# Sliding-window attention and a two-layer MLP on one core: a rewrite with other tiles, another normalisation and a scheduled order

## The chip, the cores and the metric

The kernel runs on one core of a Trainium2 chip. The metric is the device time of one execution in microseconds (us). Five engines work side by side, each through its own list of instructions in order: TensorE (PE; its weight loads are shown as PEld), VectorE (DVE), ScalarE (ACT), GpSimd (POOL) and SyncE (SP). DMA queues move data between the chip's main memory and the core's SBUF. Matmuls write to PSUM, 8 banks of 128 partitions by 2 KB.

## The reference

Inputs are q, k and v in f32, each 8 batches x 8 heads x 576 positions x 64 values, and the weights `w_in` (512 x 2048) and `w_out` (2048 x 512). Cut to what matters:

```python
scores = q @ k.T / 8
mask_plain = (rel >= 0) & (rel < 32)
mask_dil = (rel >= 0) & (rel < 128) & (rel % 4 == 0)
attn = softmax(where(mask, scores, -1e9))
x = (attn @ v) with the heads side by side
h = x @ w_in
out = maximum(0.01 * h, h) @ w_out
```

`rel` is the query's position less the key's. Heads 0 to 3 have the plain mask, heads 4 to 7 the dilated one, so a query sees 32 keys at most. There are 4608 tokens (8 x 576); the output is 4608 x 512 in f32.

## The kernel before

**Attention** (L213) takes a batch and a pair of heads at a time, 32 rounds in all. `load_and_transpose` loads 576 x 128 values of q and then of k through SP's queue in rows of 256 B, casts them to f16 on ACT (L182), transposes them with five matmuls against an identity (L185, L186) and copies them out of PSUM on DVE (L190). `load_v` (L193) has POOL clear a tile (L195), loads v by SP and casts it on ACT (L210). Scores are matmuls of 96 queries (plain) or 72 (dilated) against the 128 keys before them, one head at a time on 64 rows of the array (L236). ACT takes the exponential (L241), DVE multiplies by the mask (L248). The result times v goes into one PSUM tile (L252), and times a 128 x 64 tile of ones into another (L258), which holds the row sums on 64 partitions. DVE takes their reciprocal (L265) and multiplies (L279) into `xT`, which holds the attention's output, features on partitions.

**Weights** are loaded in f32 in the second round (L147), cast on DVE, and `w_in` is transposed (L160) and multiplied by `w_out` (L166) into `w_eff`, 0.01 of the product. The MLP uses max(h, 0.01h) = 0.99 relu(h) + 0.01h: the second part is `x @ w_eff`, without the hidden layer.

**The MLP** takes chunks of 512 tokens. An up group (L286) is four matmuls of 512 columns (L289) and then 0.99 relu on ACT (L301) or, one time in three, on DVE (L296). A down group (L306) is 16 matmuls with `w_out` (L310) and four with `w_eff` (L317), a copy on ACT (L324) and a store by SP (L325).

The order of the work is that of the program: after each round of attention at most six groups of the MLP are issued (L340), for chunks whose tokens are complete, and the rest at the end (L354).

Of the kernel before, what the change touches and what calls it, by code (L numbers as in the profile page):

```python
# [16 lines left out]
PAD = 128  # L18
POST = 128


def _mask_plain_np(S):
    krel = np.arange(128)[:, None]
    c = np.arange(S)[None, :]
    t = c // 96
    key = 96 * t - 32 + krel
    rel = c - key
    m = (key >= 0) & (rel >= 0) & (rel < WIN)
    return m.astype(np.float16)


def _mask_dil_np(S):
    krel = np.arange(128)[:, None]
    c = np.arange(S)[None, :]
    rem = c % 144
    tau = rem // 72
    ql = rem % 72
    uq = 72 * tau + ql
    uk = 72 * tau - 32 + krel
    m = (uk >= 0) & ((uq - uk) >= 0) & ((uq - uk) < WIN)  # L40
    return m.astype(np.float16)


class _QTile:

    __slots__ = (
        "half", "jl", "w", "ecol", "kstart", "kstep", "kcnt",
        "qstart", "qstep", "vslice",
    )

    def __init__(self, half, jl, w, ecol, kstart, kstep, kcnt, qstart, qstep, vslice):
        self.half = half
        self.jl = jl
        self.w = w
        self.ecol = ecol
        self.kstart = kstart
        self.kstep = kstep
        self.kcnt = kcnt
        self.qstart = qstart
        self.qstep = qstep  # L60
        self.vslice = vslice


def _plain_qtiles():
    res = []
    for t in range(6):
        res.append(
            _QTile(
                half=t // 3, jl=t % 3, w=96, ecol=96 * t,
                kstart=PAD + 96 * t - 32, kstep=1, kcnt=128,  # L70
                qstart=PAD + 96 * t, qstep=1, vslice=t,
            )
        )
    return res


def _dil_qtiles():
    res = []
    for r in range(4):
        for tau in range(2):  # L80
            j = 2 * r + tau
            res.append(
                _QTile(
                    half=r // 2, jl=2 * (r % 2) + tau, w=72,
                    ecol=144 * r + 72 * tau,
                    kstart=PAD + 4 * (72 * tau - 32) + r, kstep=4, kcnt=128,
                    qstart=PAD + 4 * (72 * tau) + r, qstep=4, vslice=j,
                )
            )
    return res  # L90
# [3 lines left out]
def kernel(  # L94
# [7 lines left out]
    out: bass.AP,  # L102
):
    nc = tc.nc
    ctx.enter_context(nc.allow_low_precision("fp16 intermediates, 1e-3 rel tol"))

    B, H, S, D = q.shape
    assert H == 8 and D == 64 and S == 576, (B, H, S, D)
    NTOK = B * S
    DMODEL = H * D  # L110
    DFF = moe_w_in.shape[1]
    NH = H // 2
    QTW = PAD + S + POST
    SCALE = float(1.0 / np.sqrt(D))

    plain_qt = _plain_qtiles()
    dil_qt = _dil_qtiles()

    mask_plain_d = nc.inline_tensor(_mask_plain_np(S), name="mask_plain").ap()
    mask_dil_d = nc.inline_tensor(_mask_dil_np(S), name="mask_dil").ap()  # L120

    cst = ctx.enter_context(tc.tile_pool(name="cst", bufs=1))
    big = ctx.enter_context(tc.tile_pool(name="big", bufs=1))
    ld = ctx.enter_context(tc.tile_pool(name="ld", bufs=2))
    att = ctx.enter_context(tc.tile_pool(name="att", bufs=2))
    epool = ctx.enter_context(tc.tile_pool(name="epool", bufs=3))
    moe = ctx.enter_context(tc.tile_pool(name="moe", bufs=2))
    pat = ctx.enter_context(tc.tile_pool(name="pat", bufs=5, space=bass.MemoryType.PSUM))
    pmo = ctx.enter_context(tc.tile_pool(name="pmo", bufs=3, space=bass.MemoryType.PSUM))

    ident = cst.tile([128, 128], FP16)
    make_identity(nc, ident)
    maskpl = cst.tile([128, S], FP16)
    nc.sync.dma_start(maskpl, mask_plain_d)
    maskdl = cst.tile([128, S], FP16)
    nc.sync.dma_start(maskdl, mask_dil_d)
    ones64 = cst.tile([128, 64], FP16)
    nc.gpsimd.memset(ones64, 1.0)

    n_fc = DMODEL // 128  # L140
    n_j = DFF // 128
    w_in_sb = big.tile([128, n_fc, DFF], FP16)
    w_out_sb = big.tile([128, n_j, DMODEL], FP16)

    w_eff_sb = big.tile([128, n_fc, DMODEL], FP16)

    def load_weights():  # L147
        for i in range(n_fc):
            wtmp = ld.tile([128, DFF], FP32, tag="wtmp_in")
            nc.sync.dma_start(wtmp, moe_w_in[i * 128:(i + 1) * 128, :])  # L150
            nc.vector.tensor_copy(out=w_in_sb[:, i, :], in_=wtmp)
        for j in range(n_j):
            wtmp2 = ld.tile([128, DMODEL], FP32, tag="wtmp_out")
            nc.sync.dma_start(wtmp2, moe_w_out[j * 128:(j + 1) * 128, :])
            nc.vector.tensor_copy(out=w_out_sb[:, j, :], in_=wtmp2)
        wT = big.tile([128, n_j, n_fc, 128], FP16)
        for j in range(n_j):
            tpw = pat.tile([128, 512], FP16, tag="ps", name="tpw")
            for i in range(n_fc):
                nc.tensor.transpose(tpw[:, 128 * i:128 * i + 128],  # L160
                                    w_in_sb[:, i, j * 128:(j + 1) * 128], ident)
            nc.scalar.copy(out=wT[:, j, :, :], in_=tpw[:, 0:512])  # L162
        for i in range(n_fc):
            weps = pat.tile([128, DMODEL], FP32, tag="ps", name="weps")
            for j in range(n_j):
                nc.tensor.matmul(weps, wT[:, j, i, :], w_out_sb[:, j, :],  # L166
                                 start=(j == 0), stop=(j == n_j - 1))
            nc.scalar.activation(out=w_eff_sb[:, i, :], in_=weps,
                                 func=AF.Copy, scale=0.01)

    xT = big.tile([128, n_fc, NTOK], FP16)

    def load_and_transpose(b, hp, src, tag):
        qld = ld.tile([128, 5, 128], FP32, tag=f"{tag}_ld")
        nc.gpsimd.memset(qld[64:128, 4, :], 0.0)  # L175
        for hh in range(2):
            h = 2 * hp + hh
            srcap = src[b, h, 0:512, :].rearrange("(T p) d -> p T d", p=128)
            nc.sync.dma_start(qld[:, 0:4, 64 * hh:64 * hh + 64], srcap)  # L179
            nc.sync.dma_start(qld[0:64, 4, 64 * hh:64 * hh + 64], src[b, h, 512:576, :])  # L180
        qldh = ld.tile([128, 5, 128], FP16, tag=f"{tag}_ldh")
        nc.scalar.copy(out=qldh, in_=qld)  # L182
        tp = pat.tile([128, 1024], FP16, tag="ps")
        for T in range(4):
            nc.tensor.transpose(tp[:, 128 * T:128 * T + 128], qldh[:, T, :], ident)  # L185
# [27 lines left out]
    def attention(b, hp):  # L213
# [11 lines left out]
        for half in range(2):  # L225
            sps = [pat.tile([128, 512], FP32, tag="ps", name="sps") for _ in range(2)]
            for qtile in qtiles:
                if qtile.half != half:
                    continue
# [52 lines left out]
    def moe_chunk_groups(tok0, ntok):  # L282
# [45 lines left out]
        for j in range(n_j):  # L328
            yield mk_j(j)
# [56 lines left out]
```

The softmax here doesn't subtract the row's maximum and nothing guards it: scores larger than these inputs give would overflow.

## Time and profile before

| | |
|---|---|
| median of 3 runs | 439.18 us (438.53 to 440.29) |
| span of the profiled execution, from its first to its last instruction | 436.9 us |
| instructions | 7886 |
| PE, DVE, ACT, POOL busy | 90%, 56%, 48%, 15% of the span |
| data moved by DMA | 50.11 MB in 137320 packets |

The profile gives the profiled execution by its span. The median is 2.3 us above it: what lies before the first instruction and after the last. Matmuls overlap, so a busy PE says that some matmul is under way. In tables of groups the columns are line, engine, operation, output and inputs with shapes, count | busy time in us, mean ns of one | idle time of the engine before them and what ended it.

### The profile page before, as it was taken

To read this page: it belongs to the slowest core of one execution; us is meant where nothing else is said; L and a number is where in the kernel's file an instruction comes from. 1 tells how busy PE (TensorE), PEld (TensorE's weight loads), DVE (VectorE), ACT (ScalarE), POOL (GpSimd) and SP (SyncE) were. 2 spreads that over 40 slices of the span, in tenths; PEclk is the share of its full clock that TensorE was granted. 3 is DMA by queue.
4 is the path that set the end of the run, shared out by engine and by line. 5 is a ranking of instruction groups with operands and counts; after the bars stand their busy time and mean duration, and the time that the engine had idled before them with its cause. 6 is when DMAs were issued, how large, how long until landed. Compare 5 with 4: busy or idle time off the path is not lost.

```text
span 436.9 us, 7886 instructions
## 1 busy us (share of the span) xinstructions
PE 392.7 (90%) x2768; PEld 193.7 (44%) x2768; DVE 244.9 (56%) x321; ACT 207.7 (48%) x412; POOL 67.6 (15%) x263
## 2 busy tenths in 40 slices
PE   1344975699999999999999999999999999999996
PEld 1223433344444544454454444445445444444442
DVE  0573326787667657756775678567766765200200
ACT  2504554464467447744764475457446521422411
POOL 4300112112112112211221121112110000000000
PEclk9996995699999999999999999999999999999999
DMA  5857766553555555635654554455441001001001
GB/s 119 255 185 251 225 165 145 115 123 78 153 130 113 142 151 134 149 107 131 153 115 114 140 118 99 132 135 118 120 122 53 2 26 48 26 25 66 7 24 74
DMA packets 137320, 50.11 MB, mean 115 GB/s; under 512 B 129856, under 2 KB 130112, under 8 KB 136768
## 3 DMA queue, kind: packets, MB, share of 16 engines
q1 hardware_dynamic: 137280, 49.61, 43.5%
q8 instruction: 22, 0.36, 0.3%
q14 instruction: 18, 0.15, 0.1%
HBM read 40.14 MB, written 9.44 MB: 113 GB/s over the span
## 4 chain that ended last, share of the span: by engine, by line
PE 82%; DVE 5%; ACT 4%; DMA 3%; SPq 3%; issue 2%; ACTq 0%; POOL 0%; POOLq 0%; DVEq 0%
PE ops L310 29%; PE hps L289 27%; PE ops L317 7%; PE opair L252 4%; PE tp L185 3%; PE sps L236 3%; PE den L258 3%; PE weps L166 2%; DVE bc_sb L265 2%; PE tp L186 2%; ACT eraw L241 2%; DMA wtmp<-in_moe_w_in_dram 2%; ACT wT L162 1%; SPq L179 1%; DVE em L248 1%
## 5 line engine op out<-in xcount | busy, mean ns | idle before, releaser
L289 PE MATMUL hps<-xT,w_in_sb 128*128 128x512 f16 x576 | 138.3, 386 | 5.4 <-DVE xT L279 4.7
L310 PE MATMUL ops<-w_out_sb,gt 128*128 128x512 f16 x576 | 135.0, 380 | 0.0
L265 DVE RECIPROCAL bc_sb<-den 128x288 f16<-128x288 f32 x64 | 120.6, 1926 | 19.3 <-PE den L258 19.1
L310 PEld LDWEIGHTS <-gt 128*128 128x128 f16 x576 | 53.5, 98 | 65.0 <-issue 3.1
L289 PEld LDWEIGHTS <-w_in_sb 128*128 128x128 f16 x576 | 52.3, 99 | 66.1 <-issue 10.6
L301 ACT ACTIVATE gt<-hps 128x512 f16<-128x512 f32 x99 | 58.9, 604 | 43.7 <-PE hps L289 43.5
L324 ACT COPY osb<-ops 128x512 f32<-128x512 f32 x36 | 21.1, 585 | 106.8 <-PE ops L317 106.8
L182 ACT CAST qldh<-qld 128x640 f16<-128x640 f32 x64 | 45.0, 730 | 23.6 <-DMA qld<-in_q_dram 10.0
L296 DVE TENSOR_SCALAR gt<-hps 128x512 f16<-128x512 f32 x45 | 30.8, 686 | 44.2 <-PE hps L289 44.2
L241 ACT ACTIVATE eraw<-sps 128x288 f16<-128x288 f32 x128 | 42.4, 419 | 22.0 <-PE sps L236 21.8
L190 DVE COPY qt<-tp 128x576 f16<-128x576 f16 x64 | 27.6, 454 | 36.8 <-PE tp L186 36.7
L210 ACT CAST v<-vld 128x512 f16<-128x512 f32 x64 | 37.6, 631 | 13.0 <-issue 9.4
L195 POOL MEMSET vld<- 128x512 f32 x64 | 33.2, 526 | 59.0 <-ACT v L210 56.9
L317 PE MATMUL ops<-w_eff_sb,xT 128*128 128x512 f16 x144 | 37.0, 379 | 0.0
L185 PE MATMUL tp<-ident,qldh 128*128 128x128 f16 x256 | 26.4, 229 | 11.5 <-ACT qldh L182 8.2
L175 POOL MEMSET qld<- 64x128 f32 x64 | 13.3, 207 | 151.0 <-ACT qldh L182 127.6
L279 DVE TENSOR_TENSOR xT<-opair,bc_sb 128x288 f16<-128x288 f32 x64 | 34.2, 604 | 0.0
L252 PE MATMUL opair<-em,v 128*64 128x72 f16 (+1 forms) x448 | 25.4, 208 | 7.4 <-DVE em L248 4.6
L252 PEld LDWEIGHTS <-v 128*64 128x64 f16 x448 | 20.3, 114 | 20.5 <-DVE em L248 14.4
L248 DVE TENSOR_TENSOR em<-eraw,maskdl 128x576 f16<-128x576 f16 x32 | 13.2, 455 | 28.3 <-ACT eraw L241 28.3
L185 PEld LDWEIGHTS <-qldh 128*128 128x128 f16 x256 | 18.4, 101 | 22.3 <-ACT qldh L182 8.5
L248 DVE TENSOR_TENSOR em<-eraw,maskpl 128x576 f16<-128x576 f16 x32 | 13.2, 455 | 23.8 <-ACT eraw L241 22.2
(25 smaller groups left out, 185.0 us busy)
## 6 DMA issues: line engine op xcount, KB each, us to landing
out_dram<-osb SPq DMA_DIRECT2D x36, 256.0 KB
qld<-in_q_dram SPq DMA_DIRECT2D x64, 128.0 KB
qld<-in_k_dram SPq DMA_DIRECT2D x64, 128.0 KB
vld<-in_v_dram SPq DMA_DIRECT2D x32, 160.0 KB
wtmp<-in_moe_w_in_dram SPq DMA_DIRECT2D x4, 1024.0 KB
wtmp<-in_moe_w_out_dram SPq DMA_DIRECT2D x16, 256.0 KB
vld<-in_v_dram SPq DMA_DIRECT2D x32, 104.0 KB
vld<-in_v_dram SPq DMA_DIRECT2D x32, 96.0 KB
```

The source lines that it names most:

```text
L182: nc.scalar.copy(out=qldh, in_=qld)
L185: nc.tensor.transpose(tp[:, 128 * T:128 * T + 128], qldh[:, T, :], ident)
L195: nc.gpsimd.memset(vld, 0.0)
L210: nc.scalar.copy(out=v1, in_=vld)
L241: nc.scalar.activation(out=eraws[hh][:, half * 288:half * 288 + 288], in_=sps[hh][:, 0:288], func=AF.Exp, scale=SCALE,)
L252: nc.tensor.matmul(opair[qtile.half][r0:r0 + 64, ocols], v1s[hh][:, qtile.vslice, :], ecols, start=True, stop=True,)
L265: nc.vector.reciprocal(out=bc_sb[:, half, :], in_=den[half][:, 0:288])
L279: nc.vector.tensor_tensor(out=outap, in0=opair[half][:, 0:288], in1=bc_sb[:, half, :], op=ALU.mult)
L289: nc.tensor.matmul(hps[:, 0:ntok], w_in_sb[:, i, j * 128:(j + 1) * 128], xT[:, i, tok0:tok0 + ntok], start=(i == 0), stop=(i == n_fc - 1),)
L301: nc.scalar.activation(out=gt[:, j, 0:ntok], in_=hps[:, 0:ntok], func=AF.Relu, scale=0.99)
L310: nc.tensor.matmul(ops[0:ntt, :], gt[:, j, tt:tt + ntt], w_out_sb[:, j, :], start=(j == 0), stop=False,)
L317: nc.tensor.matmul(ops[0:ntt, :], xT[:, i, tok0 + tt:tok0 + tt + ntt], w_eff_sb[:, i, :], start=False, stop=(i == n_fc - 1),)
```

## The change

The kernel is written anew.

- **Loads cast to f16.** q, k, v and both weights are loaded by DMAs that POOL issues and that turn f32 into f16 on the way, in rows of 256 B for q, k and v. Of batch 0 the first 96 tokens of each residue (see below) come in f32 rows of 1 KB through SP's and ACT's queues and are cast on DVE and ACT.
- **Tokens are kept by residue.** Position 4u + s is stored as (s, u). A unit of work covers 2 x 96 queries of two heads, 384 columns; a batch and a pair of heads has three units. There are 96 units.
- **The whole array.** q of two heads stands block-diagonal in `qbd`, with zeros beside it, so that one matmul over 128 rows gives the scores of both heads. v stands beside 64 columns of ones, so that one matmul gives the output on 64 partitions and the row sums on the other 64.
- **1/x as Exp(-Ln x)**, two passes on ACT. One set of ACT tables is loaded at the start.
- **The MLP** has no `w_eff`: ACT's Prelu with alpha 0.01 gives max(h, 0.01h). Its chunks are 384 tokens, 12 of them; chunks 3m and 3m + 1 need the first two units of every pair of heads of batches 2m and 2m + 1, chunk 3m + 2 the third units of both. The copy of the result goes to DVE.
- **The order** is not that of the program: each piece of work becomes a task with an engine, a time, a delay, its predecessors and a priority, and a list scheduler, run while the kernel is built, puts the tasks in order of their planned starts. Buffers used in turn ("rings") are predecessors too.

The core of the diff (lines removed are those printed above):

```diff
+    UK = U + PADK
+    tpb = [bank("tp", FP16)]
+    sps = [bank(f"sps{i}") for i in range(1)]
+    ops = [bank(f"ops{i}") for i in range(2)]
+    hps = [bank(f"hps{i}") for i in range(2)]
+    fps = [bank(f"fps{i}") for i in range(2)]
...
+    def load(queue, dst, src, n, size, deps=(), issue=None):
+        eng = {"SP": nc.sync, "ACTQ": nc.scalar, "POOL": nc.gpsimd}[queue]
+        cost = {"SP": 0.5, "ACTQ": 0.5, "POOL": 1.0}[queue] if issue is None else issue
+        return dma(queue, cost, rate(n, size), deps,
+                   lambda: eng.dma_start(dst, src))
...
+                tp.append(load("POOL", at(vp[slot], p0, p1, 0, [128, 24], [1, D]),
+                               dram(v, b * H * HS + (s - 32) * D,
+                                    [4 * D, 32], [96 * D, 24], [1, D]),
+                               768, 256, deps_p))
+        for tau in range(2):
+            for h in range(4):
+                td.append(load("POOL",
+                               at(vd[slot], 0, 128, (h * 2 + tau) * 512, [128, 4], [1, D]),
+                               dram(v, (b * H + 4 + h) * HS + tau * 16 * 4 * D,
+                                    [4 * D, 128], [D, 4], [1, D]),
+                               512, 256, deps_d))
+        v_ready[b] = (tp, td)
...
+        for half in range(2) if b == 1 else (2,):
+            h0, hn = (4 * half, 4) if half < 2 else (0, 8)
+            for name, src, dst in (("q", q, qn), ("k", k, kn)):
+                ts = [load("POOL", at(dst[slot], 0, 128, s * 512 + h0 * D, [D, hn], [1, D]),
+                           dram(src, (b * H + h0) * HS + s * D, [4 * D, 128], [HS, hn], [1, D]),
+                           128 * hn, 256, deps) for s in range(4)]
+                for i in ((half,) if half < 2 else (0, 1)):
+                    got[name, i] = ts
+            if half != 1:
+                for name, src, p0 in (("q", q, 0), ("k", k, 64)):
+                    got[name, "l"] = load(
+                        "POOL", at(lf[slot], p0, p0 + 64, 0, [D, H], [1, D]),
+                        dram(src, b * H * HS + 512 * D, [D, 64], [HS, H], [1, D]),
+                        512, 256, deps)
...
+        for name, src, dst, queue in (("q", q, q0f, "SP"), ("k", k, k0f, "ACTQ")):
+            t_f32[name, hp] = load(
+                queue, at(dst, 0, 96, hp * 512, [256, 2], [1, 256]),
+                dram(src, 2 * hp * HS, [4 * D, 96], [HS, 2], [1, 256]), 192, 1024)
...
+    def ones(i):
+        t_ones["p", i] = pool_op(
+            lambda: nc.gpsimd.memset(at(vp[i], 0, 128, D, [128, 24], [1, D]), 1.0), 1.5)
+        t_ones["d", i] = pool_op(
+            lambda: nc.gpsimd.memset(at(vd[i], 0, 128, D, [128, 32], [1, D]), 1.0), 2.0)
...
+    cuts = [0, 128, 256, 512, 1024, 1536, 2048]
...
+    for n in range(len(cuts) - 1):
+        load_w_in(n)
+        if n == 2:
...
+    load_qk(1, [])
+    load_v(1, [], [])
+    ones(1)
+    for n in range(4):
+        t = load("POOL", at(w_out, 0, 128, n * 4 * DM, [DM, 4], [1, DM]),
+                 dram(moe_w_out, n * 4 * 128 * DM, [DM, 128], [128 * DM, 4], [1, DM]),
+                 512, 2048)
+        for j in range(4 * n, 4 * n + 4):
+            w_out_t[j] = t
+    ones(2)
...
+                def pe(src=src, tp=tp, pos=pos, lanes=lanes, to=to, tw=tw):
+                    nc.tensor.transpose(
+                        at(tp, 0, 128, to + 128, [tw, 4], [1, 32]),
+                        lf[lanes][:, hp * 128:hp * 128 + 128],
+                        con[:, 128 * pos:128 * pos + 128])
+                    for s in range(4):
+                        nc.tensor.transpose(
+                            tp[:, to + s * tw:to + s * tw + 128],
+                            src[lanes][:, s * 512 + hp * 128:s * 512 + hp * 128 + 128],
+                            ident)
...
+                                out=at(qbd[slot], 64 * hh, 64 * hh + 64, hh * S, [1, S]),
+                                in_=at(tp, 64 * hh, 64 * hh + 64, 0, [1, S]))
...
+                    ka = at(kt[slot], 0, 128, 128 * t, [1, 128])
+                    qa = at(qbd[slot], 0, 128, 24 * t, [S, 2], [U, 4], [1, 24])
+                nc.tensor.matmul(st[:, 192 * i:192 * i + 192], ka, qa, start=True, stop=True)
...
+                  lambda: nc.scalar.activation(out=et, in_=st[:, 0:384], func=AF.Exp, scale=SCALE),
+                  prio + 0.1)
...
+                        va = at(vp[b % NV], 0, 128, (h * 6 + t) * 128, [1, 128])
+                    c = 192 * i + 96 * hh
+                    nc.tensor.matmul(ot[:, c:c + 96], va, et[:, c:c + 96],
+                                     start=True, stop=True)
...
+        t_l = add("ACT", 0.37, 0.2, [t_v] + r_old,
+                  lambda: nc.scalar.activation(out=rt, in_=ot[64:128, 0:384], func=AF.Ln),
+                  prio + 0.2)
...
+        t_r = add("ACT", 0.37, 0.2, [t_l],
+                  lambda: nc.scalar.activation(out=rt, in_=rt, func=AF.Exp, scale=-1.0),
+                  prio + 0.2)
...
+                    out=at(xt[m % 2], p0, p0 + 64, base + e, *o_),
+                    in0=at(ot, 0, 64, c, *i_), in1=at(rt, 0, 64, c, *i_), op=ALU.mult)
...
+            for i in range(NI):
+                nc.tensor.matmul(ht[:, 0:384],
+                                 w_in[:, i * DFF + j * 128:i * DFF + j * 128 + 128],
+                                 at(xt[m % 2], 0, 128, i * 1152 + x0, [1, 384]),
+                                 start=(i == 0), stop=(i == NI - 1))
...
+                  lambda: nc.scalar.activation(out=gt[c % 2][:, j * 384:j * 384 + 384],
+                                               in_=ht[:, 0:384], func=AF.Prelu, alpha=0.01),
...
+                for j in range(4 * p, 4 * p + 4):
+                    nc.tensor.matmul(ft, gt[c % 2][:, j * 384 + tt * 128:j * 384 + tt * 128 + 128],
+                                     w_out[:, j * DM:j * DM + DM],
+                                     start=(j == 0), stop=(j == NJ - 1))
...
+        t_c = add("DVE", 0.62, 0.25, [pieces[-1]] + o_old,
+                  lambda: nc.vector.tensor_copy(out=ob, in_=ft), -1000)
...
+        for p0, tok, n in rows(c, tt):
+            dep = [t_c]
+            o_users.append(load("SP", dram(out, tok * DM, [4 * DM, n], [1, DM]),
+                                ob[p0:p0 + n, :], n, 2048, dep))
...
+    order = plan.run()
...
+    with tc.manual_schedule():
+        nc.scalar.preload_act_table_set("natural_log_exp_and_others")
+        for t in order:
+            t.fn()
```

## Rows read from the trace of the kernel before

**Rows 1.** Busy time by stretch: columns named in the second line

```profile
core 0: us, PE busy (x) PEld busy (x) DVE busy (x) ACT busy (x) POOL busy (x), PEclk, DMA share, GB/s
0.00:88.00 88.00, 48.71 (x370) 27.09 (x370) 42.24 (x59) 36.41 (x71) 17.44 (x69) 0.86 0.66 183
88.00:433.00 345.00, 343.77 (x2400) 166.56 (x2398) 202.68 (x263) 170.70 (x340) 50.11 (x194) 1.00 0.39 98
...
66.00:77.00 11.00, 5.22 (x50) 3.02 (x51) 7.66 (x9) 5.13 (x10) 2.86 (x11) 0.53 0.65 146
11.00:22.00 11.00, 4.00 (x41) 2.73 (x41) 6.70 (x10) 6.00 (x14) 3.72 (x14) 1.00 0.85 257
```

**Rows 2.** The chain of waits, 28 to 76 us: start, us, what

```profile
30.00 7.41 DMA wtmp<-in_moe_w_in_dram
...
45.07 10.67 PE weps L166 x48
```

**Rows 3.** The chain of waits, 333 to 437 us: start, us, what

```profile
343.61 0.24 PE den L258 x2
...
344.82 0.22 PE tp L185 x4
345.05 0.13 PE tp L186
...
350.06 0.65 PE sps L236 x16
...
352.12 0.38 PE opair L252 x8
...
371.03 13.81 PE hps L289 x64
384.84 3.45 PE ops L310 x16
388.29 0.86 PE ops L317 x4
```

**Rows 4.** Groups of instructions, shapes kept apart

```profile
L265 DVE RECIPROCAL bc_sb<-den 128x288 f16<-128x288 f32 x64 | 120.6, 1926 | 19.3 <-PE den L258 19.1
...
L301 ACT ACTIVATE gt<-hps 128x512 f16<-128x512 f32 x99 | 58.9, 604 | 43.7 <-PE hps L289 43.5
...
L279 DVE TENSOR_TENSOR xT<-opair,bc_sb 128x288 f16<-128x288 f32 x64 | 34.2, 604 | 0.0
L195 POOL MEMSET vld<- 128x512 f32 x64 | 33.2, 526 | 59.0 <-ACT v L210 56.9 <-DMA qld<-in_q_dram 2.2
L296 DVE TENSOR_SCALAR gt<-hps 128x512 f16<-128x512 f32 x45 | 30.8, 686 | 44.2 <-PE hps L289 44.2
L190 DVE COPY qt<-tp 128x576 f16<-128x576 f16 x64 | 27.6, 454 | 36.8 <-PE tp L186 36.7
...
L248 DVE TENSOR_TENSOR em<-eraw,maskdl 128x576 f16<-128x576 f16 x32 | 13.2, 455 | 28.3 <-ACT eraw L241 28.3
...
L182 ACT ACT_TABLE_LOAD x1 | 1.3, 1283 | 5.6 <-DMA qld<-in_q_dram 5.6
```

**Rows 5.** Timeline of SP's queue, 5 to 16 us: start, us, what

```profile
5.77 0.51 SPq L180 DMA_DIRECT2D qld<-in_k_dram  x1
6.33 0.59 SPq L179 DMA_DIRECT2D qld<-in_q_dram  x1
```

**Rows 6.** The page's part on DMA queues: packets, MB, share of 16 engines

```profile
q1 hardware_dynamic: 137280, 49.61, 43.5%
```

**Rows 7.** Timeline of ACT, 340 to 343 us: start, us, what, idle before

```profile
341.27 1.32 ACT L241 ACTIVATE eraw<-sps 128x288 f16<-128x288 f32 x4 [0.93 <-PE sps L236]
```

**Rows 8.** Timeline of the last microseconds: start, us, what

```profile
433.27 0.58 ACT L324 COPY osb<-ops 128x512 f32<-128x512 f32 x1 [3.73 <-PE ops L317]
433.88 0.33 SPq L325 DMA_DIRECT2D out_dram<-osb  x1
```

More of the change, by code (lines that the diff above doesn't have):

```diff
@@ L9 @@
 from concourse._compat import with_exitstack
-from concourse.masks import make_identity
 FP16 = mybir.dt.float16
@@ L44 @@
[L44 to L74, printed above, removed]
@@ L113 @@
-    QTW = PAD + S + POST
+    NP = H // 2
+    NI = DM // 128
+    NJ = DFF // 128
+    U = S // 4
     SCALE = float(1.0 / np.sqrt(D))
[L116 to L124, printed above, removed]
@@ L135 @@
[L135 to L169, printed above, removed]
@@ new lines, with load_w_in @@
+    t_vz = pool_op(lambda: nc.gpsimd.memset(vp[0][:, 0:D], 0.0), 0.2)
+    load_v(0, [t_vz], [])
+    t_ones = {}
+    def ones(i):
[3 more added lines that the diff above has]
+            lambda: nc.gpsimd.memset(at(vd[i], 0, 128, D, [128, 32], [1, D]), 1.0), 2.0)
+    ones(0)
+    cuts = [0, 128, 256, 512, 1024, 1536, 2048]
+    def load_w_in(n):
+        a, z = cuts[n], cuts[n + 1]
+        t = load("POOL", at(w_in, 0, 128, a, [DFF, NI], [1, z - a]),
+                 dram(moe_w_in, a, [DFF, 128], [128 * DFF, NI], [1, z - a]),
+                 512, 4 * (z - a))
+        for j in range(a // 128, z // 128):
+            w_in_t[j] = t
@@ new lines, with attend @@
+    for i in range(8):
+        add("PE", 0.43, 0.0, [t_warm],
+            lambda: nc.tensor.matmul(fps[0], warm[:, 0:128], warm, start=True, stop=True), -900)
+    def attend(b, part, units):
+        for hp in range(NP):
+            pr = rank(b, part, hp)
+            ev = transposes(b, hp, "all" if b else part, pr)
+            for u in units:
+                unit(b, hp, u, ev, pr)
+    acts_of, downs_of = {}, {}
+    for m in range(B // 2):
+        for b in (2 * m, 2 * m + 1):
+            if b >= 2:
+                load_qk(b, users_load.get(b - NQK, []))
+                load_v(b, users_v.get(b - NV, []), users_v.get(b - NV, []))
+            attend(b, 0, (0, 1, 2) if b else (0, 1))
+            if b == 0:
+                attend(0, 1, (2,))
+        x_free[m + 2] = []
+        for kind in range(3):
+            c = 3 * m + kind
+            acts = acts_of[c] = []
+            x_free[m + 2] += [up(c, j, acts) for j in range(NJ)]
+            gt_free[c] = downs_of[c] = []
+            for tt in range(3):
+                down(c, tt, acts, downs_of[c])
```

663 lines of the change are left out of this document (442 added, 221 removed).

## The prediction

> **What bounds the kernel now.** I read the busy time by stretch first. From 88 us on PE is busy for 343.77 of 345 us at the full granted clock of 1.00; DVE has 202.68 and ACT 170.70 [rows 1]. The chain of waits agrees: in that stretch it is almost nothing but matmuls, 64 of an up stage in 13.81 us, 16 of a down group in 3.45 us, so 215.7 ns for 512 columns with no gap [rows 3]. So a faster DVE alone would not move the end; fewer PE columns would. The first 88 us are another matter: PE is busy for 48.71 us of them, and its clock sinks to 0.53 between 66 and 77 us, about the lower level of 1.2 GHz, where it is busy less than half the time [rows 1]. There the chain goes through a weight load (7.41 us) and the 10.67 us of 48 matmuls for `w_eff` [rows 2]. The time is therefore a start of 88 us in which little PE work fits, 345 us of full PE, a tail of 4 us, and 2.3 us outside the span (436.9 against the median of 439.18).
>
> **PE's work after the change.** Prices by column come from [rows 3].
> - Up: 192 groups of four matmuls of 384 columns. 215.8 ns x 384/512 = 161.9 ns, so 124.3 us; the columns are those of before.
> - Down: 144 pieces of four matmuls, 36 x 3.45 = 124.2 us, as before.
> - Gone: 144 matmuls with `w_eff` (0.86 us for four: 31 us), the 64 that make it (222 ns each: 14 us) with their transposes (64 at 57 ns: 4 us), and 128 row-sum matmuls (0.12 us each: 15 us). Together 64 us.
> - Transposes: 28 rounds with ten, four rounds of batch 0 with sixteen. Four take 0.22 us now and the odd fifth 0.13; with 0.35 for five that is 19.6 us and, with 64 at 57 ns, 3.6 us.
> - Scores: 96 units of 384 columns. Sixteen of 72 columns take 0.65 us now, 41 ns each, but two heads run on two halves of the rows. The new form streams one head's zeros under the other's values, so it pays for all columns: 384/512 x 215.8 = 162 ns, 15.5 us.
> - Values: 80 units with four matmuls of 96 columns, 16 with eight of 48. Eight of 72 take 0.38 us, 47 ns each, so 0.19 and 0.38 us: 21 us. That the weights are twice as wide is unpriced in the trace; with a 128-column transpose as the upper price, 57 ns, it is 4.5 us more.
>
> Sum: 308 us. The steady part of before holds 343.77 us of PE and the whole 392.66; the new whole is less than the old steady part.
>
> **The other engines, beside PE.** ACT gets 96 Exp, 96 Ln, 96 Exp and 192 Prelu, all of 384 columns. Four Exps of 288 take 1.32 us [rows 7], so by proportion 0.44 us for 384: 211 us. DVE gets 96 copies out of PSUM at 454 ns, 96 masks at not more than 455, 192 products at not more than 604 and 36 copies at about 686 [rows 4]: at most 228 us. Both stay under PE's 308, but ACT, near 75% of the steady part, is the next in line. Where ACT is late, up groups wait for PSUM (below).
>
> The 64 reciprocals cost 1,926 ns each for 288 columns [rows 4], 6.7 ns a column. Kept on DVE for 96 units of 384 they would be 247 us, on top of 228: DVE would be the bound at about 475 us. Two passes on ACT are 0.88 us a unit. The Trainium skill, "ScalarE: Activation LUTs", section "What it computes", says to leave reciprocals to VectorE. By that rule this kernel would end near 490 us, by the rows it is better not followed here; the new kernel doesn't use ScalarE's own reciprocal, about whose accuracy the page warns.
>
> **The loads, and the start.** This is the part that the trace doesn't show: no DMA of before is issued by POOL, and none casts. What must arrive before the first down group can begin, in POOL's order: v of batch 0 (20 DMAs, 7,136 rows), `w_in` (6, 3,072), the rest of batch 0's q and k (8, 4,096), q and k of batch 1 (18, 9,216), its v (12, 7,168), `w_out` (4, 2,048). That is 68 DMAs with 32,736 rows. Batches 2 to 7 have 22 DMAs with 16,384 rows each; in all 131,040 rows.
> - POOL's time, lower end: SP's price, 0.51 to 0.59 us a DMA whether it has 64 rows or 512 [rows 5]: 68 x 0.55 = 37 us. Upper end: POOL works through a DMA row by row. Its memset takes 526 ns for 512 elements a partition, 1.03 ns an element [rows 4]. With four such steps a row it would be 4.1 ns, 135 us. I take two steps, one for the source and one for the destination: 2.06 ns a row, 67 us. In the queue stand also the memsets of ones (3,584 elements a batch buffer, two of them before `w_out`) and of 512 zeros, 7.9 us. With 2.7 us to land (the last store leaves at 434.2, the span ends at 436.9 [rows 8]), `w_out` is there at about 78 us.
> - The DMA engines' time: 137,280 packets took 43.5% of 16 engines over 436.9 us [rows 6], so 22.1 ns on one and 1.38 ns on all 16. 27,616 small rows take 38 us; 10.0 MB of weights and f32 rows at the best rate seen, 257 GB/s [rows 1], 39 us: 77 us. If all 17 MB went at 257 GB/s it would be 66 us.
>
> I take 72 us, between 66 and 78. Before that PE can do batch 0's attention (8 us), chunk 0's up stage (10.4 us) and what has come of batch 1's attention (about 4 us): 22 us. Values also wait for the ones, which stand behind 20 DMAs. The remaining 286 us then run without a load in the way, if POOL keeps ahead: a batch's 16,384 rows are 33.8 us of POOL and 22.6 us of the DMA engines, against 308/8 = 38.5 us of PE. The cover is 5 us thin on POOL; if it goes, POOL is late next.
>
> **Sum.** 72 + 286 = 358 us; the last copy (0.69 us, by L296's price), four stores of 0.33 us at SP and 2.7 us to land: 363 us of span; with 2.3 us outside, **365 us**. The PSUM clearings, the masks' load and the eight casts of batch 0 lie in the wait for the loads and cost nothing; without that wait the casts would be some 4 us of ACT and DVE.
>
> **Rivals.**
> 1. *POOL is the bound, and the kernel is slower.* Place: POOL's queue, all through. After batch 7's loads come its attention (12 us), chunks 10 and 11 (41 us) and the tail (5 us), so the time is 75.6 us (with memsets of 11.6, landing, start and 2.3 outside) plus 131,040 times the price of a row. It passes 439 us from 2.8 ns a row on, 2.7 steps of the memset's; at four steps it is 615 us. For it: nothing in the trace excludes four steps, and the rows are many and short. Against: SP's issue hardly grows from 64 rows to 512 [rows 5]. Chance 0.15. The Trainium skill, "DMA: Bandwidth & Descriptors", sections "Issuing engine by pattern" and "SWDGE vs HWDGE vs iDMA", speaks against the change here: descriptors of a DMA issued by GpSimd are computed by a program on its cores, one pair per operation, and the path of SP and ACT is generally faster, though only GpSimd's can cast. No run here shows such a DMA yet.
> 2. *PE waits in its order.* There are two banks for up groups where three were shared, one for scores and one for transposes. An up group takes 0.65 us and its Prelu some 0.5 (L301 takes 604 ns for 512 columns [rows 4]); with an Exp or Ln of 0.44 in front of it the bank is late by about 0.25 us. If that meets half of the 192 groups it is 24 us, 389 us in all; down pieces and attention between two up groups speak against it. Chance 0.14.
> 3. *The loads come faster.* Half as many bytes are written as read. With everything 1.4 times as fast `w_out` would land near 52 us, and the time be 345 us. Against: only rates up to 257 GB/s are seen. Chance 0.15.
> 4. *The single set of tables doesn't hold.* If Prelu were not in the set of Exp and Ln, each change would cost a table load of 1,283 ns [rows 4]; two for each of 192 Prelus are 493 us on ACT, so about 700 us. Chance 0.02.
>
> **Chances.** The forecast (357 to 380 us) 0.52, a time between 405 and 437 us 0.02. Faster by over 0.5% (about what a measurement of this kernel can tell from no change): 0.52 + 0.15 + 0.14 + 0.02 = 0.83. Slower: 0.15 and most of 0.02, so 0.16; 0.01 between. The range takes in rivals 2 and 3 and the bounds of the start, 335 to 420 us; it leaves out rivals 1 and 4 and a little below 335.
>
> **What would show it.** Right: PE below five tenths until some 70 us, then nine, clock 1.00; the first down matmul (512 columns with `w_out`) at 70 to 80 us; up matmuls at 162 ns and down at 216 in the chain; PE's busy time near 310 us; one table load; DVE and ACT each under 80%. The forecast is wrong if PE pauses for loads in every batch, with POOL's queue full throughout (rival 1), if its chain shows Prelu before up groups (rival 2), or if the first down matmul comes before 55 us (rival 3).

## The result and the profile after

The changed kernel takes **356.55 us** (median of 4 runs, 356.06 to 357.09), the kernel before in the same session 439.74 us (438.53 to 441.66): a ratio of 0.8112, interval 0.8087 to 0.8137. The profiled execution took 356.06 us, its span 354.3.

From the page: busy time by engine, then PE's busy share and its granted clock in 40 slices, each in tenths.

```profile
PE 320.3 (90%) x2368; PEld 191.4 (54%) x2368; DVE 174.4 (49%) x446; ACT 228.9 (65%) x485; POOL 161.1 (45%) x212
...
PE   4446866689999999999999999999999999999994
...
PEclk9555995599999999999999999999999999999999
```

Busy time by stretch, which answers to [rows 1]:

```profile
core 0: us, PE busy (x) PEld busy (x) DVE busy (x) ACT busy (x) POOL busy (x), PEclk, DMA share, GB/s
0.00:20.00 20.00, 9.87 (x58) 5.48 (x59) 10.66 (x30) 5.67 (x10) 16.34 (x28) 0.71 1.18 135
20.00:40.00 20.00, 11.82 (x80) 7.25 (x78) 8.77 (x27) 12.18 (x27) 15.98 (x22) 0.61 1.28 139
40.00:60.00 20.00, 14.40 (x131) 10.10 (x130) 12.07 (x33) 11.78 (x26) 18.97 (x25) 0.82 1.67 100
60.00:80.00 20.00, 15.07 (x118) 9.23 (x118) 12.77 (x36) 14.89 (x33) 16.28 (x19) 0.75 1.37 151
...
77.40:346.00 268.60, 268.60 (x1988) 159.41 (x1986) 131.32 (x327) 185.52 (x394) 95.03 (x123) 1.00 0.96 79
```

The picture is that of before with less of it: a start in which PE has gaps and a low clock, and then a stretch in which PE is busy without a gap. In it ACT has 185.52 of 268.60 us (69%), DVE 49%. In the start the granted clock falls to 0.50, the lower level of 1.2 GHz, in stretches where PE is idle for a large part of the time (10 to 30 us, where it is busy 8.80 of 20 us, and parts of 50 to 70, where it is busy 11.73 of 20). The start is about 77 us instead of 88, the full stretch 272 us instead of 345.

The chain of waits at the seam (start, us, what):

```profile
68.58 8.44 DMA qn<-in_q_dram
...
77.06 0.36 PE ops L536 x8
...
79.15 1.30 PE hps L607 x8
80.45 0.86 PE fps L646 x4
```

Eight up matmuls take 1.30 us (162 ns each), four down matmuls 0.86. The step that names the load of `qn` at 68.58 is an inference from semaphores: the matmul at 77.06 reads no q, and DVE's products of an earlier unit, whose output bank it may reuse, end at 76.91 us. So the chain's way through the start is taken with care below. The end, from the timeline:

```profile
337.79 11.39 PE L646 MATMUL fps<-w_out,gt 128*128 128x512 f16 x52
...
349.21 0.69 DVE L654 COPY osb<-fps 128x512 f32<-128x512 f32 x1 [2.76 <-DMA out_dram<-osb]
```

The last matmul ends at 349.18 us and the last copy starts right behind it.

Groups that answer to [rows 4, 7] (busy, mean ns, idle before):

```profile
L614 ACT ACTIVATE gt<-hps 128x384 f16<-128x384 f32 x192 | 93.4, 490 | 69.3 <-PE hps L607 67.0
L513 ACT ACTIVATE ee<-sps 128x384 f16<-128x384 f32 x96 | 46.8, 487 | 14.9 <-PE sps L508 14.4
L565 ACT ACTIVATE rc<-ops 64x384 f32<-64x384 f32 x96 | 46.1, 486 | 15.2 <-PE ops L551 11.4
L568 ACT ACTIVATE rc<-rc 64x384 f32<-64x384 f32 x96 | 49.2, 519 | 2.0
L586 DVE TENSOR_TENSOR xt<-ops,rc 64x192 f16<-64x192 f32 x192 | 67.1, 349 | 37.3 <-ACT rc L568 34.7
```

The reciprocal of one unit of 384 columns is now 486 + 519 ns on ACT.

### The profile page after: what moved, and what is told of

The parts are those of the page before. It is cut to its first block, busy times and chain, and to the rows that moved or that the text cites. A ratio compares the mean times of both kernels' runs of the same rounds, so it can differ in the third digit from the quotient of the medians.

```text
span 354.3 us, 6469 instructions
## 1 busy us (share of the span) xinstructions
PE 320.3 (90%) x2368; PEld 191.4 (54%) x2368; DVE 174.4 (49%) x446; ACT 228.9 (65%) x485; POOL 161.1 (45%) x212
## 4 chain that ended last, share of the span: by engine, by line
PE 76%; POOL 12%; DMA 10%; DVE 0%; issue 0%; SPq 0%; POOLq 0%
PE fps L646 33%; PE hps L607 32%; DMA w_in<-in_moe_w_in_dram 4%; POOL vd L233 3%; PE tp L397 3%; PE ops L551 3%; PE sps L508 3%; DMA qn<-in_q_dram 2%; DMA vp<-in_v_dram 2%; POOL vp L233 2%; POOL vd L319 1%; POOL qn L233 1%; POOL vp L317 1%; POOL kn L233 1%; POOL w_out L233 1%; POOL w_in L233 1%
## 5 line engine op out<-in xcount | busy, mean ns | idle before, releaser
L607 PE MATMUL hps<-xt,w_in 128*128 128x384 f16 x768 | 153.5, 330 | 1.3 <-DVE xt L586 1.2
L646 PE MATMUL fps<-w_out,gt 128*128 128x512 f16 x576 | 146.2, 381 | 0.0
L614 ACT ACTIVATE gt<-hps 128x384 f16<-128x384 f32 x192 | 93.4, 490 | 69.3 <-PE hps L607 67.0
L607 PEld LDWEIGHTS <-w_in 128*128 128x128 f16 x768 | 72.2, 99 | 48.8 <-issue 4.2
L586 DVE TENSOR_TENSOR xt<-ops,rc 64x192 f16<-64x192 f32 x192 | 67.1, 349 | 37.3 <-ACT rc L568 34.7
L513 ACT ACTIVATE ee<-sps 128x384 f16<-128x384 f32 x96 | 46.8, 487 | 14.9 <-PE sps L508 14.4
L565 ACT ACTIVATE rc<-ops 64x384 f32<-64x384 f32 x96 | 46.1, 486 | 15.2 <-PE ops L551 11.4
L527 DVE TENSOR_TENSOR ee<-ee,con 128x384 f16<-128x384 f16 x96 | 34.3, 358 | 42.7 <-ACT ee L513 40.9
L233 POOL DMA_DIRECT2D vd<-in_v_dram x64 | 47.5, 747 | 9.1 <-DMA vp<-in_v_dram 2.1
L568 ACT ACTIVATE rc<-rc 64x384 f32<-64x384 f32 x96 | 49.2, 519 | 2.0
```

What stands on the lines that cost most here:

```text
L233: lambda: eng.dma_start(dst, src))
L513: lambda: nc.scalar.activation(out=et, in_=st[:, 0:384], func=AF.Exp, scale=SCALE),
L527: nc.vector.tensor_tensor(out=io, in0=io, in1=mk, op=ALU.mult)
L565: lambda: nc.scalar.activation(out=rt, in_=ot[64:128, 0:384], func=AF.Ln),
L568: lambda: nc.scalar.activation(out=rt, in_=rt, func=AF.Exp, scale=-1.0),
L586: nc.vector.tensor_tensor(out=at(xt[m % 2], p0, p0 + 64, base + e, *o_), in0=at(ot, 0, 64, c, *i_), in1=at(rt, 0, 64, c, *i_), op=ALU.mult)
```

## The experiments

The notes on the runs call a unit of 384 score columns a "round"; a batch has twelve. (In the prediction a round of transposes is a pair of heads, three units.) Ratios are to the kernel before. Line numbers shift a little where lines were added or removed.

### Is PE's column work the bound from 77 us on?

**extra144** adds 144 matmuls of 512 columns with a zero operand, one in each down piece.

```diff
+                    if j % 4 == 2:
+                        nc.tensor.matmul(ft, warm[:, 0:128], warm, start=False, stop=False)
```

> Four more matmuls of 512 columns, with zero weights and zero inputs, in each of the 36 down groups: the 144 matmuls that the kernel before had with w_eff, in work though not in data. Planned order unchanged. Theory (from 77 us on PE's columns set the end): 144 x 215.7 ns = 31.1 us, so 387 to 389 us. Rival (PE only looks busy, and ACT or the loads set the pace): less than 10 us, so under 367 us.

386.45 us, ratio 0.8782 (0.8756 to 0.8808): 29.9 us more, against 31.1 for 144 x 215.8 ns, and half a microsecond under the range expected. The stretch behind the start is as full as in the changed kernel:

```profile
77.00:379.00 302.00, 301.26 (x2150) 174.49 (x2149) 132.51 (x329) 187.91 (x397) 94.57 (x123) 1.00 0.86 72
```

Columns put on PE come out at the end nearly one for one. So about 30 of the 83 us gained can be put down to the 144 matmuls with `w_eff`; the other PE work that the change leaves out was not put back piece by piece.

**no_late_loads** leaves out the loads of q, k and v of batches 4 to 7 (their units read what the buffers still hold).

```diff
-            if b >= 2:
+            if 2 <= b < 4:
                 load_qk(b, users_load.get(b - NQK, []))
...
+            elif b >= 4:
+                qk_ready[b], v_ready[b] = qk_ready[b - NQK], v_ready[b - NV]
```

> The loads of q, k and v of batches 4 to 7 are left out, so their attention is computed from the data of batches 1 to 3 and the output of these batches is not the reference's. 65,536 of 131,040 rows go. Theory (after the start the loads lie beside PE and cost nothing): 355.5 to 357.5 us. Rival (POOL's DMAs hold up DVE or PE in the steady part): 5 us or more faster, under 351.5 us.

356.57 us (356.33 to 356.93): no difference. The same 79 us in the changed kernel and in this one:

```profile
107.00:186.00 79.00, 79.00 (x665) 49.38 (x663) 53.27 (x138) 67.90 (x146) 70.08 (x90) 1.00 2.10 144
```

```profile
107.00:186.00 79.00, 79.00 (x664) 49.35 (x662) 53.58 (x138) 67.92 (x146) 1.75 (x3) 1.00 0.20 38
```

68 us of POOL's work and 106 GB/s go, and PE is at 79.00 of 79.00 in both. The loads of batches 4 to 7 are hidden whole.

### What the reciprocal and the order are worth

**recip_dve** makes the reciprocal one instruction of DVE.

```diff
-        t_l = add("ACT", 0.37, 0.2, [t_v] + r_old,
-                  lambda: nc.scalar.activation(out=rt, in_=ot[64:128, 0:384], func=AF.Ln),
-                  prio + 0.2)
-        t_r = add("ACT", 0.37, 0.2, [t_l],
-                  lambda: nc.scalar.activation(out=rt, in_=rt, func=AF.Exp, scale=-1.0),
-                  prio + 0.2)
+        t_r = add("DVE", 2.55, 0.2, [t_v] + r_old,
+                  lambda: nc.vector.reciprocal(out=rt, in_=ot[64:128, 0:384]),
+                  prio + 0.2)
```

> Ln and Exp(-) on ACT are replaced by one reciprocal on DVE per unit; its time is given to the scheduler, so the order is made anew. By the row of before (1,926 ns for 288 columns, 6.7 ns a column) 96 reciprocals of 384 columns add 247 us to the 174 us of DVE. Theory (DVE becomes the bound): DVE busy about 421 us, time 430 to 455 us, PE with gaps. Rival (reciprocals hide beside PE as they did before): 355 to 365 us.

523.67 us (522.90 to 524.47), ratio 1.1904 (1.1864 to 1.1945): slower than the kernel before, and by far more than was expected. The page, then waits (us in total, times, longest):

```profile
PE 357.6 (69%) x2368; PEld 206.7 (40%) x2368; DVE 409.0 (78%) x542; ACT 141.2 (27%) x293; POOL 160.4 (31%) x212
...
L565 DVE RECIPROCAL rc<-ops 64x384 f32<-64x384 f32 x96 | 241.6, 2539 | 6.7 <-PE ops L551 4.4
```

```profile
PE sps L508 <- DVE kt L468: 50.9, 12, 6.7
...
DVE osb L651 <- PE fps L643: 36.1, 5, 18.5
```

The reciprocal costs 2,539 ns, 6.6 ns a column against 6.7 in [rows 4], and it is the longest line of the chain of waits (27%). But DVE is busy for only 409.0 us of 521.1. The expectation took the busiest engine's sum for the time; here PE waits for DVE in some stretches and DVE for PE in others, and PE's work itself gets longer: 357.6 us of busy time at a mean clock of 0.80, against 320.3 at 0.94.

**program_order** emits the work in the order in which the program makes it.

```diff
-    order = plan.run()
+    plan.run()
+    order = plan.tasks
```

> The tasks are issued in the order in which the program makes them, not in the scheduler's: two batches of attention, then three chunks, and so on. Theory (the order hides the chain of a unit behind MLP matmuls): a unit's chain is about 1.4 us with one bank of scores and two of outputs against some 0.5 us of PE work, so 96 x 0.9 = 86 us and more where the clock sinks: 435 to 465 us. Rival (engines find overlap without it): under 370 us.

662.43 us, ratio 1.5060 (1.5013 to 1.5107): the direction was right, the size far off. PE's longest wait in total, and two units in a row in a stretch of attention:

```profile
PE ops L551 <- DVE ee L527: 121.3, 78, 2.1
```

```profile
560.02 0.48 PE L551 MATMUL ops<-ee,vp 128*128 128x96 f16 x4 [0.97 <-DVE ee L527]
...
560.29 0.52 PE L508 MATMUL sps<-qbd,kt 128*128 128x192 f16 x2
...
562.76 0.48 PE L551 MATMUL ops<-ee,vp 128*128 128x96 f16 x4 [1.95 <-DVE ee L527]
```

A unit takes 2.74 us, of which PE works 0.8 (560.02 to 560.81). PE executes its list in order, so without the interleaving nothing stands behind a waiting unit. This is the largest single effect measured here, 306 us against the changed kernel, with the same buffers and banks. The prediction's sum had taken the order for granted: it added PE's work behind the start as if nothing could stand in its way, and its rival on the order (rival 2) asked only for waits at the up banks, 24 us.

### What sets the 77 us of the start?

First theory: POOL's queue. **ones_dve** moves the memsets of ones from POOL to DVE; **w_sp_dve** and **w_sp_act** load the weights in f32 by SP in 32 pieces and cast them on DVE or ACT; **both_act** is the first and the last together.

```diff
-        t_ones["p", i] = pool_op(
-            lambda: nc.gpsimd.memset(at(vp[i], 0, 128, D, [128, 24], [1, D]), 1.0), 1.5)
...
+        t_ones["p", i] = add(
+            "DVE", 1.65, 0.2, after,
+            lambda: nc.vector.memset(at(vp[i], 0, 128, D, [128, 24], [1, D]), 1.0), -980 + 900 * i)
...
+        t = load("SP", wsv, src, n, size, staged[k - NW:k - NW + 1] if k >= NW else [])
+        fn = lambda: nc.scalar.copy(out=dst, in_=wsv)
+        staged.append(add("ACT", 0.5, 0.2, [t], fn, prio))
...
-        t = load("POOL", at(w_in, 0, 128, a, [DFF, NI], [1, z - a]),
```

> The memsets of ones move from POOL to DVE; batch 0's run at the start, those of the other two buffers once the v of the batch before has been loaded. POOL's queue loses 6.4 us before w_out. Theory (the start is set by POOL's queue, one issue after another): full PE from about 71 us instead of 77, 349 to 352 us. Rival (the start is set by the DMA engines or by batch 1's attention, and POOL only waits beside them): 355 to 358 us.

> Both weights are loaded in f32 through SP's queue, in 32 pieces of 256 KB over six buffers, and cast on DVE, as the kernel before did. POOL's queue loses 10 DMAs (7.7 us) and some waits behind w_in (about 5 us). Theory (POOL's queue): 343 to 350 us. Rival (DMA engines): 355 us or more. If DVE's casts from SBUF to SBUF hold up POOL, this one is slower than the same with casts on ACT by 3 us or more.

> As the run before, but the 32 casts (about 0.6 us each) are on ACT. Theory (POOL's queue): 343 to 350 us, within 3 us of the casts on DVE unless those hold up POOL; ACT has 19 us more work in a start in which it is half idle. Rival (DMA engines): 355 us or more.

> Ones on DVE and weights through SP with casts on ACT. Theory (POOL's queue): the two savings add up, 337 to 346 us, full PE from 58 to 66 us. Rival: after the first saving something else (batch 1's attention, 12 units of 1.4 us or more) sets the start, and the second gives less than 2 us.

361.10, 366.50, 366.19 and 365.68 us: all slower than 356.55, by 4.5 to 10 us; for the first, neither the theory nor the rival had put the time above 358. Each edit put something in front of an engine's list. In ones_dve, DVE's timeline has the memsets ahead of the casts that batch 0 waits for; the first cast starts at 8.74 us, in the changed kernel at 4.99, and PE stands 4.2 us for it, where it stood 0.5:

```profile
5.33 1.34 DVE L319 MEMSET vp<- 128x1536 f16 x1 [0.27 <-issue]
7.05 1.76 DVE L322 MEMSET vd<- 128x2048 f16 x1 [0.38 <-issue]
8.74 1.06 DVE L414 CAST qn<-q0f 96x512 f16<-96x512 f32 x3
```

In w_sp_act, ACT's casts wait for one piece after the other, 1.5 us apart, and an attention step behind them waits with them; PE then stands for 9.49 us:

```profile
26.62 0.62 ACT L333 CAST w_in<-wst 128x512 f16<-128x512 f32 x1 [0.89 <-DMA wst<-in_moe_w_in_dram]
...
29.64 0.62 ACT L333 CAST w_in<-wst 128x512 f16<-128x512 f32 x1 [0.89 <-DMA wst<-in_moe_w_in_dram]
30.28 0.87 ACT L575 ACTIVATE rc<-ops 64x384 f32<-64x384 f32 x2
```

```profile
32.53 0.48 PE L518 MATMUL sps<-qbd,kt 128*128 128x192 f16 x2 [9.49 <-ACT ee L523]
```

In w_sp_dve, PE stands 5.58 us behind one of DVE's casts. It took 4.12 us, the middle one of the sixteen for `w_in` 0.42; POOL wrote its ones in the same stretch:

```profile
20.69 4.12 DVE L333 CAST w_in<-wst 128x512 f16<-128x512 f32 x1 [1.31 <-DMA wst<-in_moe_w_in_dram]
```

```profile
21.38 1.40 POOL L317 MEMSET vp<- 128x1536 f16 x1
22.70 1.83 POOL L319 MEMSET vd<- 128x2048 f16 x1
```

No run tells whether the memsets held the cast up. So these runs refute "less on POOL is faster", but don't measure POOL's share cleanly, as each brought a wait of its own; that these waits are what each kernel lost is read from the rows, not tested.

The three runs that load the weights by SP show one thing more. Their first down matmul comes at 46 to 52 us, in the changed kernel at 68.08, and still they are slower. PE in w_sp_act:

```profile
50.00:70.00 20.00, 20.00 (x164) 12.15 (x163) 10.41 (x30) 14.43 (x32) 16.36 (x19) 1.00 1.71 152
70.00:90.00 20.00, 10.96 (x109) 8.32 (x107) 14.31 (x40) 14.51 (x33) 17.81 (x24) 0.61 1.88 118
```

It is full from 50 to 70 us, mostly with chunk 0, and then idle for 9 of 20 us while batch 1's units run by themselves, as no other chunk can begin without them. An early `w_out` alone doesn't end the start; the units of batch 1 have to be through as well.

Next theories: the pace of batch 1's units (one score bank), or the planned order. **sps2** gives the scores two banks and the down tiles one (the last chunk's tiles use score banks); **durs** puts measured durations into the plan; **sps2_durs** does both.

```diff
-    sps = [bank(f"sps{i}") for i in range(1)]
+    sps = [bank(f"sps{i}") for i in range(2)]
...
-    fps = [bank(f"fps{i}") for i in range(2)]
+    fps = [bank(f"fps{i}") for i in range(1)]
...
-        cost = {"SP": 0.5, "ACTQ": 0.5, "POOL": 1.0}[queue] if issue is None else issue
+        cost = {"SP": 0.57, "ACTQ": 0.57, "POOL": 0.9 if n == 1024 else 0.74}[queue]
...
-        t_e = add("ACT", 0.37, 0.2, [t_s] + e_old,
+        t_e = add("ACT", 0.487, 0.2, [t_s] + e_old,
```

> Theory S: what holds PE up until 77 us is the chain of batch 1's twelve attention rounds, not the weights or POOL. In the changed kernel the rounds between 62 and 74 us come in pairs 3.28 us apart: ACT works 2.8 us of that (two Exp, two Ln, two Exp(-)), and 0.57 us of a pair it waits for the second scores, since there is only one score bank and PE waits 1.75 us for the Exp that empties it. A second score bank (taken from the two banks of the down matmuls; the last chunk's tiles use the score banks, which are free by then) takes that 0.5 us off each pair in the stretches where nothing else fills PE, some five to eight pairs: 2 to 4 us less, 352.5 to 354.5 us, with pairs near 2.8 us apart. Rival D: loads set the start; the pairs get closer but PE fills no earlier, 356 to 357 us. Rival F: one bank for the down matmuls makes PE wait for its copy (0.69 us) between tiles in the steady part; then slower, 358 us or more, and PE has gaps after 80 us.

> Theory O: the order itself is what the start loses to. The scheduler plans Exp, Ln and Prelu at 0.37 us where the trace shows 0.49 to 0.52, products at 0.29 where it shows 0.35, a POOL load at 1.0 where it shows 0.74; an engine works its queue in order, so what was planned too early stands in front of what is ready. With the measured durations in the plan and nothing else changed, the idle time of PE before 77 us (26 us) falls by 2 to 6 us: 350.5 to 354.5 us. Rival: the order is no loss, as the chain of rounds (theory S) or the loads set the start whatever the order: 356 to 357.5 us, and PE is full from 76 to 78 us as before.

> Both edits. If S and O both hold, and what they gain is not the same idle time, 348 to 352.5 us; if only one holds, its own result; if neither, 356 to 358 us. Where S holds, the pairs of batch 1's rounds are bound by ACT alone, at 2.8 us a pair.

sps2: 363.32 us (362.42 to 363.75). Its score matmuls from 64.31 to 71.83 us are five units apart in 7.5 us, 1.5 us each against 1.64, so the bank does shorten the unit, yet the kernel loses 6.8 us. Rival F has the time right (358 us or more), but the wait that it names shows only once, 0.52 us at 81.76; behind 85 us PE waits for 0.2 us in all. PE has 2.2 us less done between 70 and 90 us, part of it at a lower clock; first the changed kernel, then sps2:

```profile
70.00:80.00 10.00, 8.96 (x75) 4.99 (x75) 7.10 (x20) 7.36 (x16) 6.28 (x9) 1.00 1.94 175
80.00:90.00 10.00, 10.00 (x65) 5.72 (x64) 1.75 (x4) 4.75 (x10) 8.16 (x12) 1.00 2.33 164
```

```profile
70.00:80.00 10.00, 7.29 (x55) 3.59 (x53) 5.85 (x17) 7.54 (x17) 6.83 (x10) 0.82 1.99 173
80.00:90.00 10.00, 9.48 (x57) 5.20 (x56) 2.13 (x6) 4.16 (x9) 7.45 (x11) 1.00 2.40 133
```

Whether the single down bank or the changed order does that is not settled. With measured durations in the plan 4 us come back: sps2_durs takes 359.35 us (357.78 to 360.27), above every range expected of it.

durs: 356.47 us (356.04 to 357.64): no difference, as its rival said, with a different order on every engine but POOL and SP. PE's longest wait in it is new:

```profile
PE ops L551 <- POOL vp L317: 7.0, 2, 6.6
```

The better plan asks for batch 1's values earlier, and then POOL has not yet put the ones beside them.

Last, **quarter_w** loads a quarter of both weights and uses it four times, so that the loads come early without anything being moved.

```diff
-    cuts = [0, 128, 256, 512, 1024, 1536, 2048]
+    cuts = [0, 128, 256, 512]
...
-    for n in range(4):
+    for n in range(1):
         t = load("POOL", at(w_out, 0, 128, n * 4 * DM, [DM, 4], [1, DM]),
...
-                                 w_in[:, i * DFF + j * 128:i * DFF + j * 128 + 128],
+                                 w_in[:, i * DFF + j % 4 * 128:i * DFF + j % 4 * 128 + 128],
```

> Leaves out three quarters of both weight loads (3 of 6 DMAs of w_in and 3 of 4 of w_out; the matmuls use the loaded quarter four times), so POOL has 6 issues less (4.7 us) and the DMA engines 6 MB less to read before 77 us; every other instruction stays. Theory A, which is left after the runs so far: PE fills when batch 1's q, k, v and ones have arrived (60.9 us in the changed kernel) and its rounds have run, and POOL's issue and the DMA engines' drain hold these up about alike, so that taking the one away (memsets of ones, or weights, moved elsewhere) only lengthens the waits for the other. Here both shrink: batch 1's ones end at 52 to 55 us, PE is full from 67 to 72 us, and the time is 346 to 351 us. Rival C: the pace of the rounds and the order set it; arrivals come earlier and nothing else does: 354.5 to 357 us, PE full from 75 to 78 us.

357.82 us (356.94 to 359.04), ratio 0.8124 (0.8101 to 0.8147): not faster. POOL and PE in the changed kernel, then in quarter_w:

```profile
57.76 1.40 POOL L317 MEMSET vp<- 128x1536 f16 x1
...
60.83 3.01 POOL L233 DMA_DIRECT2D w_out<-in_moe_w_out_dram  x4
...
60.64 0.85 PE L551 MATMUL ops<-ee,vp 128*128 128x96 f16 x8
...
68.08 1.91 PE L646 MATMUL fps<-w_out,gt 128*128 128x512 f16 x4
```

```profile
51.06 1.40 POOL L317 MEMSET vp<- 128x1536 f16 x1
...
54.12 0.77 POOL L233 DMA_DIRECT2D w_out<-in_moe_w_out_dram  x1
...
63.11 0.26 PE L393 MATMUL tp<-con,lf 128*128 128x128 f16 x1 [1.03 <-DVE qbd L448]
...
63.60 0.84 PE L552 MATMUL ops<-ee,vp 128*128 128x96 f16 x8
...
71.04 1.91 PE L647 MATMUL fps<-w_out,gt 128*128 128x512 f16 x4
```

The ones of batch 1 are there 6.7 us earlier, and its first values run 3 us later: in PE's list they stand behind all of batch 1's transposes, which wait for DVE's copies (1.03 us in the row above), and the plan, made anew, begins these transposes later, at 50.18 us against 48.49. `w_out`'s first load is issued 6.7 us earlier too, and the first down matmul comes 3 us later. PE is busy for 9.96 us between 70 and 80, so it fills in the stretch that theory A named, but with less behind it: by 80 us it has been busy for 51.03 us, in the changed kernel for 51.16, and 271.83 us are left against 269.18. (The profiled execution of quarter_w took 359.04 us, the longest of its five.) The time lies above both ranges, nearer to rival C's. With durs the reading is that **two limits stand at about the same height**: order the units earlier, and PE waits for POOL; bring the loads earlier, and PE waits in its order. Shown are the two halves; a kernel with both edits at once, earlier loads and the plan with measured durations, was not tried, so how much of the 77 us it would take stays open.

## Why the prediction was right, and where it was off

- **The bound.** Right. PE busy without a gap at clock 1.00 behind the start, fewer PE columns as the gain; extra144 shows it from the other side.
- **PE's work.** Forecast 308 us. Up and down matmuls cost what was forecast (162 and 216 ns, 248.5 us in all). The attention of a pair of heads takes 1.61 us (38.5 us of the chain between 77 and 349 us, for the 24 pairs of batches 2 to 7), forecast (308 - 248.5)/32 = 1.86. So the sum is about 248.5 + 32 x 1.61 = 300 us, 8 less. Two terms were too dear: five transposes take 0.28 us in the chain, not 0.35, and the values of a unit 0.17 us (0.21 with eight matmuls of 48 columns), not 0.19 (0.38). The 4.5 us for weights twice as wide were named beside the sum and not added to it; a values matmul of 96 columns takes 43 ns, so nothing of them can be seen. The profile's busy time of 320.3 is longer because in the start PE is busy for 48.2 us with about 28 us of work at these prices: up matmuls at the low clock take 320 ns (thirteen in 4.16 us, at 31.87), and eight matmuls on zeros at the very start, 3.6 us that the sum left out, are among it.
- **The other engines.** ACT was forecast at 211 us and took 228.9: a pass over 384 columns takes 486 to 519 ns, not 440. It was off the path all the same, at 69% behind the start where 75% was forecast. DVE took 174.4 us, under its bound of 228.
- **POOL's queue: the step that was mis-sized.** The prediction took 2.06 ns a row, 67 us for the 68 DMAs up to `w_out`, from a memset's price. They took 48.12 us. The price is mostly per DMA, and the total lies nearer its lower end of 37 us than the 67 taken:

```profile
L233 POOL DMA_DIRECT2D vd<-in_v_dram x48 | 35.6, 747 | 8.9 <-DMA vp<-in_v_dram 2.1 <-PE hps L607 1.6 <-PE ops L551 1.0
L233 POOL DMA_DIRECT2D kn<-in_k_dram x20 | 17.7, 930 | 0.0
```

  The first row is of DMAs with 512 rows, 747 ns each, the second of DMAs with 1,024, 930 ns: 0.36 ns a row on about 0.56 us, or 1.47 ns a row with all in (48.12 us for 32,736). With 6.9 us of memsets (forecast 7.9) POOL is busy for 55.05 of the 63.77 us until the last `w_out` is issued; of the other 8.7 us it waits 8.0 for earlier loads to land. (The first eight loads go out without a wait; from then on each waits until the load eight places before it has landed, as the loads of this program carry eight semaphores in turn.) Those waits were not in the sum; they give back 8.7 of the 20 us by which the queue was priced too long. Later on 90 issues take 70.08 us, so a batch's 22 take some 17 us and with their waits about 20, against 34 forecast: the cover that was called 5 us thin is about 18 us thick.
- **The start.** Forecast: `w_out` there at 72 us, 22 us of PE done, then no gap. The first down matmul comes at 68.08 us, inside 66 to 78, and from there to 77.06 PE is idle for 1.05 of 8.98 us; after that it has no gap. By 77.06 about 28 us of work are done (300 - 272), some 21 of them before 68.08, an estimate from PE's 7.9 busy us in between. So 49 us are lost in the start, forecast 72 - 22 = 50, and 77 + 272 = 349 us stand against 358. The size came out; the reason given for it, that the start ends when `w_out` has landed, did not. The first down matmul follows the scores before it without a wait; in quarter_w `w_out` is issued 6.7 us earlier and the first down matmul comes 3 us later; in w_sp_act it comes at 49.12 us and the kernel is slower. The start ends when batch 1's units are through as well, in an order fixed in advance. That the number was hit with this reason wrong is in part luck.
- **The tail.** 5.1 us from the last matmul, 349.2, to the end; forecast 5. 1.8 us lie outside the span; taken 2.3.
- **Rival 1** (POOL the bound) fails by its own threshold: 1.47 ns a row with all in, against 2.8. The path through POOL is slower than SP's, 0.75 against 0.51 to 0.59 us [rows 5] for one issue. The Trainium skill, "DMA: Bandwidth & Descriptors", section "Issuing engine by pattern", calls the other path generally faster; the trace agrees for an issue, and no_late_loads shows that the loads of batches 4 to 7 cost the kernel nothing.
- **Rival 2** (PE waits for up banks): no wait of PE behind 77.06 us, though Prelu took 490 ns, close to what that rival assumed. The prediction's own reason, that downs and attention stand between the ups, fits; program_order shows what happens to PE in attention when nothing stands between.
- **Rival 3** (loads faster): POOL's 68 DMAs were 1.4 times as fast as taken, half of its case (the DMA engines had to be faster too), but POOL waited for landings, and `w_out`'s four loads, issued from 60.83 us on, landed 5.8 to 12.0 us after their issue, not near 52 us. Where the first down matmul did come before 55 us, in the three runs with the weights on SP, the time was 366 us and not 345.
- **Rival 4**: one table load of 1,283 ns in the whole run.
- **The signs.** Up and down prices, the single table load, and ACT and DVE under 80% came as written down. The first down matmul, at 68.08 us, is a little before the 70 to 80 named; PE's busy time is 320.3 us and not near 310; and PE is not below five tenths until 70 us: its row shows 6 and 8 from 27 us on.
- **The reciprocal.** Forecast for the DVE variant near 490 us; measured 523.67. The sum (DVE 409 us instead of 475, as masks and products were cheaper than bounded) was too high, and the idea that the busiest engine's sum is the time made it too low; the two errors partly hid each other. The Trainium skill, "ScalarE: Activation LUTs", section "What it computes", gives the reciprocal to VectorE, since ScalarE's own function for it has accuracy issues. Ln and Exp on ACT avoid that function, and in this kernel the rule would cost 167 us.

In sum 365 us was forecast and 356.55 measured; the 8 us are the 8 us of attention that PE did not need, and what was wrong in the start cancels.

## What to carry to other kernels

Where one engine is full, price its columns first: the forecast was within 3% though its start rested on a wrong reason. PE took its list in order here, so only the order kept it full (306 us between two orders of the same work), and moving work to an "idle" engine can cost more than it frees if it lands in front of something due earlier. When two edits each show no gain, ask whether two limits stand at the same height before calling either free.

## What the chip showed that was not expected

- A DMA issued by POOL, casting from f32 to f16, costs POOL 0.75 us with 512 rows and 0.93 with 1,024: a quarter more for twice the rows.
- When SP loaded the weights beside POOL's loads, POOL's waits for landings grew enough that both_act issued batch 1's last v load at about 62.6 us, though 6 DMAs and two memsets less stood ahead of it; in the changed kernel it was 57.0 us.
- Casts of 32 weight pieces on DVE or on ACT make no difference to the time, 366.50 against 366.19 us, although one of DVE's took 4.12 us, beside POOL's memsets, where the middle one took 0.42.
- In the start the granted clock of the record and the duration of a matmul don't always go together. Between 20 and 30 us it is 0.50 in the changed kernel and 1.00 in quarter_w; two score matmuls take 0.48 us in both, and 0.33 us later on, at 1.00 in both.
